# Sending one 2 MB zero fill as 17 narrow transfers and a rest

## The chip, the cores and the metric

The kernel runs on one core of one Trainium2 chip. The metric is device time in microseconds (us). Ratios are the mean time of one kernel's runs over the mean of the other's runs of the same rounds, so they are not quite the ratios of the medians that are quoted; 95% intervals stand beside them.

## The reference, cut to what matters

The reference is one decode step of a small transformer layer (sliding-window attention over a cache, then a gated unit) with its gradients. Only the last 4096 of 32768 cache rows are read, so the gradients of both caches are zero in the first 28672 rows of each of 8 groups.

```python
k = jnp.repeat(k_cache[:, :, Sk - W:, :], rep, axis=1)     # W = 4096, Sk = 32768
v = jnp.repeat(v_cache[:, :, Sk - W:, :], rep, axis=1)
...
_out, _vjp = jax.vjp(_f, A_x, A_k_cache, A_v_cache, A_wq, A_wo, B_w_gate, B_w_up, B_w_down)
```

Writing those zeros is most of the traffic: 103 fills of 2 MB go through GpSimd's queue alone (216 MB), out of 334.76 MB in all.

## The kernel before

`zeros` is the first 8192 columns of a large on-chip array, of which only the first half stays zero throughout. A fill copies it to 2 MB of a gradient. Fills 0 to 41 read all of it. Fills 42 to 54 read the first half twice, because block 1's gate and up weights are loaded into the second half. The later fills wait for a memset that restores that half.

```python
HALF0, HALF1 = 42, 55
zeros = ar(0, ZW)                                  # ZW = 8192
wgu_off = [RB + 28 * KB, ZW // 2]                  # block 1's weights: second half of zeros
...
def send_fills(n0, n1, halves=False):
    for reg in fills[n0:n1]:
        if halves:
            ZQ.dma_start(out=reg.rearrange("p (k f) -> p k f", k=2), in_=zeros[:, 0:ZW // 2].unsqueeze(1).to_broadcast([128, 2, ZW // 2]))
        else:
            ZQ.dma_start(out=reg, in_=zeros)

send_fills(0, HALF0)
send_fills(HALF0, HALF1, True)
...                                                # attention: scores and moments of 8 groups
def load_block(n):                                 # gate: SyncE's queue, up: ScalarE's
    f0, nb, w, wgu, wd = block_views(n)
    for eng, i, wt in ((LD, 0, B_w_gate), (nc.scalar, 1, B_w_up)):
        eng.dma_start(out=wgu[:, 0:3, i, :], ...)
        eng.dma_start(out=wgu[0:DQ, 3, i, :], ...)
    LD.dma_start(out=wd, ...)

load_block(0)
load_block(1)
...
for n in range(len(BLOCKS)):                       # three blocks of the gated unit
    ...                                            # DVE's four reductions over wgu (line 428)
    if n + 2 < len(BLOCKS):
        load_block(n + 2)                          # block 2 takes block 0's place
    if n == 1:
        nc.vector.memset(ar(ZW // 2, ZW // 2), 0.0)
        send_fills(HALF1, len(fills))
```

The order of instructions on each engine is not the order of the text: a scheduler chooses it when the kernel is built. In the trace GpSimd's 103 transfers name eight semaphores in turn, and each from the ninth on is issued after the landing of the one eight places before it: the first landed at 17.57 us, and the ninth was issued at 17.86.

## Time and profile before

| | before |
|---|---|
| time, 2 runs | 798.55 and 799.08 us |
| span of the profiled run | 797.2 us |
| DMA engines' share (sum of the queues) | 99.6% |
| median time of a 16384 B packet | 611 ns |
| first and last of the 16 engines to finish | 785.9 and 795.6 us |

The page and the views that matter are shown and read in the prediction. The last row comes from the packet records. They do not name the engine, but 28,930 of the 29,365 packets start 3 or 4 ns before another one ends, so they can be strung into sixteen chains, and a chain is taken for an engine here. Where two engines end a packet within a few ns the chains can swap. Ends, idle gaps and sums over all engines are safe; what one engine did over a long time is not.

### The profile page before, as it was taken

To read this page: it belongs to the slowest core of one execution; us is meant where nothing else is said; L and a number is where in the kernel's file an instruction comes from. 1 tells how busy PE (TensorE), PEld (TensorE's weight loads), DVE (VectorE), ACT (ScalarE), POOL (GpSimd) and SP (SyncE) were. 2 spreads that over 40 slices of the span, in tenths; PEclk is the share of its full clock that TensorE was granted. 3 is DMA by queue.
4 is the path that set the end of the run, shared out by engine and by line. 5 is a ranking of instruction groups with operands and counts; after the bars stand their busy time and mean duration, and the time that the engine had idled before them with its cause. 6 is when DMAs were issued, how large, how long until landed. Compare 5 with 4: busy or idle time off the path is not lost.

```text
span 797.2 us, 7318 instructions
## 1 busy us (share of the span) xinstructions
PE 478.9 (60%) x2926; PEld 222.6 (28%) x2926; DVE 437.1 (55%) x629; ACT 196.0 (25%) x309; POOL 61.8 (8%) x112
## 2 busy tenths in 40 slices
PE   0459999999999999251409478684450553722000
PEld 0334434344344333121208334331220211310000
DVE  2116584765846782263690679579653784964000
ACT  0142314134132201010102126353330442534000
POOL 4000000010101111100210001010000000000000
PEclk9989999999999999555558779766555556765555
DMA  9999999999999999999999999999999999999995
GB/s 349 431 430 430 428 431 430 430 428 430 430 423 427 427 419 413 423 421 424 432 428 423 424 431 431 428 425 427 424 424 422 424 424 424 423 427 418 433 434 247
DMA packets 29352, 334.76 MB, mean 420 GB/s; under 512 B 2819, under 2 KB 5894, under 8 KB 7814
## 3 DMA queue, kind: packets, MB, share of 16 engines
q0 software_dynamic: 16496, 216.01, 64.0%
q1 hardware_dynamic: 11382, 116.68, 34.8%
q10 hardware_dynamic: 1440, 1.61, 0.6%
q8 instruction: 23, 0.38, 0.2%
q14 instruction: 11, 0.09, 0.0%
HBM read 53.69 MB, written 280.59 MB: 419 GB/s over the span
## 4 chain that ended last, share of the span: by engine, by line
PE 37%; DMA 32%; DVE 16%; ACT 4%; issue 2%; another core or an unknown queue 0%; SPq 0%; DVEq 0%; ACTq 0%
DMA out_dram<-arena 19%; PE M_ps L317 12%; PE ok_ps L320 7%; PE rows_ps L256 6%; PE tr_ps L253 4%; DMA dh_bc<-in_grad_out_dram 4%; DMA arena<-in_A_k_cache_dram 4%; DMA arena<-in_B_w_down_dram 3%; ACT arena L270 2%; DVE arena L635 2%; DVE arena L459 2%; PE dqb_ps L502 2%; DMA arena<-in_B_w_gate_dram 2%; DVE arena L650 2%; PE d_ps L643 2%
## 5 line engine op out<-in xcount | busy, mean ns | idle before, releaser
L312 DVE TENSOR_TENSOR arena<-arena,p_f 128x2048 bf16<-128x2048 bf16 x64 | 145.4, 2286 | 61.6 <-PE M_ps L317 61.5
L317 PE MATMUL M_ps<-arena 128*128 128x512 bf16 x512 | 128.9, 380 | 0.2 <-ACT arena L323 0.2
L643 PE MATMUL d_ps<-arena,rT 32*128 32x512 bf16 x256 | 46.6, 529 | 111.0 <-DVE arena L651 63.9
L253 PE MATMUL tr_ps<-ident_bf,arena 128*128 128x128 bf16 x1024 | 92.5, 242 | 19.6 <-ACT arena L611 11.2
L256 PE MATMUL rows_ps<-arena,vpad 128*16 128x512 bf16 x256 | 90.6, 451 | 19.9 <-DVE arena L613 14.6
L133 POOL DMA_DIRECT2D out_dram<-arena x90 | 48.6, 542 | 538.5 <-DMA out_dram<-arena 491.3
L253 PEld LDWEIGHTS <-arena 128*128 128x128 bf16 x1024 | 69.0, 108 | 73.8 <-issue 64.4
L270 ACT COPY arena<-tr_ps 128x1024 bf16<-128x1024 bf16 x64 | 61.8, 1015 | 64.7 <-PE tr_ps L253 64.7
L647 ACT CAST arena<-d_ps 128x512 bf16<-128x512 f32 x64 | 37.7, 589 | 128.4 <-PE d_ps L643 128.3
L320 PE MATMUL ok_ps<-arena 128*16 128x512 bf16 x256 | 63.8, 381 | 0.9 <-DVE arena L297 0.9
L317 PEld LDWEIGHTS <-arena 128*128 128x128 bf16 x512 | 43.3, 99 | 59.0 <-issue 23.2
L611 ACT COPY arena<-tr_ps 128x1024 bf16<-128x1024 bf16 x32 | 32.6, 1019 | 94.6 <-PE tr_ps L253 36.4
L650 DVE CAST arena<-d_ps 128x512 bf16<-128x512 f32 x64 | 43.8, 684 | 16.9 <-PE d_ps L643 16.4
L651 DVE CAST arena<-d_ps 128x512 bf16<-128x512 f32 x64 | 43.5, 679 | 11.2 <-DMA out_dram<-arena 11.2
L643 PEld LDWEIGHTS <-rT 32*128 32x128 bf16 x256 | 11.2, 96 | 136.5 <-issue 90.0
L648 ACT CAST arena<-d_ps 128x512 bf16<-128x512 f32 x64 | 38.1, 595 | 11.9 <-DMA out_dram<-arena 11.9
L635 DVE TENSOR_TENSOR arena<-R_sb,tl_f 128x4096 bf16<-128x4096 bf16 x8 | 35.4, 4419 | 0.7 <-ACT R_sb L633 0.7
L256 PEld LDWEIGHTS <-vpad 128*16 128x16 bf16 x256 | 19.1, 92 | 58.4 <-issue 51.3
L320 PEld LDWEIGHTS <-arena 128*16 128x16 bf16 x256 | 19.1, 89 | 41.6 <-issue 20.5
L514 DVE CUSTOM_DVE_ANT_0 arena<-arena 128x4096 bf16<-128x4096 bf16 x3 | 13.1, 4423 | 23.9 <-ACT arena L507 23.9
L285 ACT ACTIVATE e_f<-cols_ps,nbias 128x32 f32<-128x32 f32 x16 | 4.5, 286 | 86.8 <-DVE nbias L281 86.8
L258 DVE COPY arena<-rows_ps 16x512 f32<-16x512 f32 x16 | 10.8, 676 | 26.6 <-PE rows_ps L256 26.6
(198 smaller groups left out, 387.9 us busy)
## 6 DMA issues: line engine op xcount, KB each, us to landing
out_dram<-arena POOLq DMA_DIRECT2D x103, 2048.0 KB, 51.7
out_dram<-arena SPq DMA_DIRECT2D x18, 2048.0 KB, 32.3
arena<-in_A_v_cache_dram SPq DMA_DIRECT2D x10, 2048.0 KB, 50.0
arena<-in_A_k_cache_dram SPq DMA_DIRECT2D x8, 2048.0 KB, 29.2
out_dram<-arena SPq DMA_DIRECT2D x4, 4096.0 KB, 43.8
arena<-in_A_wq_dram SPq DMA_DIRECT2D x2, 3072.0 KB, 20.6
arena<-in_A_wo_dram SPq DMA_DIRECT2D x2, 1792.0 KB, 14.5
out_dram<-arena SPq DMA_DIRECT2D x2, 1792.0 KB, 15.1
```

The source lines that it names most:

```text
L133: ZQ.dma_start(out=reg, in_=zeros)
L253: nc.tensor.transpose(tr_ps[:, dh, i, :], X_sb[:, 4 * q + i, dh * 128:(dh + 1) * 128], ident_bf[:])
L256: nc.tensor.matmul(rows_ps[:], lhsT=pad[:, dh, 16 * q:16 * q + 16], rhs=XT[:, dh].rearrange("p t k -> p (t k)"), start=(q == 0 and dh == 0 ...
L270: sT_ps = dots(kv_at(K_off[g]), KT_slot, vpad[g % 2], rows1, ps_c, "cols", lambda q, XT, ps: nc.scalar.copy(out=XT, in_=ps))
L312: nc.vector.tensor_tensor(out=pK, in0=K_sb[:, 4 * c:4 * c + 4, :].unsqueeze(2).to_broadcast([128, 4, 2, Dh]), in1=p_f[:, c::8, :].unsqueez ...
L317: nc.tensor.matmul(M_ps[:, vh, :], lhsT=V_sb[:, t, vh * 128:(vh + 1) * 128], rhs=pK[:, i, :, :].rearrange("p h d -> p (h d)"), start=(t == ...
L320: nc.tensor.matmul(ok_ps[:].rearrange("p k d -> p (k d)"), lhsT=ppad[g % 2][:, 8 * (t % 4) + t // 4, :], rhs=both(g, t), start=(g == 0 and ...
L635: nc.vector.tensor_tensor(out=RB_, in0=R_sb[:].unsqueeze(1).to_broadcast([128, 8, 512]), in1=tl_f[:].unsqueeze(2).to_broadcast([128, 8, 51 ...
L643: nc.tensor.matmul(d_ps[:, qi].rearrange("p w d -> p (w d)"), lhsT=rT[32 * q:32 * (q + 1), :], rhs=RB_[32 * q:32 * (q + 1), l, :], start=T ...
L648: nc.scalar.copy(out=stK[:, t:t + 2, :], in_=d_ps[:, :, 1, :])
L650: nc.vector.tensor_copy(out=stV[:, t:t + 2, :], in_=d_ps[:, :, 0, :])
L651: nc.vector.tensor_copy(out=stK[:, t:t + 2, :], in_=d_ps[:, :, 1, :])
```

## The change

The diff says what it does and not why. It sends fill 4 as seven transfers of 2 rows and ten of 3 rows, of 17 different lengths (1024 to 14848 B a row, 310,784 B in all), and the rest as 128 rows of 13956 B. A likely intent is to put the DMA engines out of step with one another.

```diff
-    send_fills(0, HALF0)
+    send_fills(0, 4)
+    flat = fills[4].rearrange("p f -> (p f)")
+    base = 0
+    for k, sizes in ((2, [512 * (17 + 2 * j) // 2 for j in range(7)]), (3, [512 * (1 + j) for j in range(5)]), (3, [256 * (11 + j) for j in range(5)])):
+        span = sum(sizes)
+        view = flat[base:base + k * span].rearrange("(k s) -> k s", k=k)
+        base += k * span
+        c0 = 0
+        for w in sizes:
+            ZQ.dma_start(out=view[:, c0:c0 + w], in_=zeros[0:k, 0:w])
+            c0 += w
+    rest = (128 * ZW - base) // 128
+    ZQ.dma_start(out=flat[base:].rearrange("(p f) -> p f", f=rest), in_=zeros[:, 0:rest])
+    send_fills(5, HALF0)
     send_fills(HALF0, HALF1, True)
```

## The prediction

> **What bounds the kernel now.** I read the page first: busy shares and the slices.
>
> ```profile
> PE 478.9 (60%) x2926; PEld 222.6 (28%) x2926; DVE 437.1 (55%) x629; ACT 196.0 (25%) x309; POOL 61.8 (8%) x112
> ...
> DMA  9999999999999999999999999999999999999995
> GB/s 349 431 430 430 428 431 430 430 428 430 430 423 427 427 419 413 423 421 424 432 428 423 424 431 431 428 425 427 424 424 422 424 424 424 423 427 418 433 434 247
> ```
>
> No compute engine passes 60%, but the DMA engines are full in every slice but the last. The queue table gives 64.0 + 34.8 + 0.6 + 0.2 = 99.6% of sixteen engines' span. In the packet records a packet of 16384 B takes 611 ns in the median, 26.8 GB/s per engine and 429 GB/s for sixteen. 334.76 MB at 429 GB/s is 780 us of the 797.2 us span, so at most 17 us can be won by any change that moves the same bytes. Where are they? Adding up each packet's time above the usual time for its size gives 9 us per engine, of which 1.9 us fall in the first 20 us. The rest is mostly start and end: all sixteen engines are busy until 785 us, then 14, 10 (at 788), 3 (at 790), 2 until 794, and the last stops at 795.6 us. Their mean end is near 789.3 us. That is an uneven finish of some 6 us.
>
> Second, GpSimd's queue and its waits.
>
> ```profile
> POOL out_dram L133 <- DMA out_dram<-arena: 491.3, 75, 9.6
> POOL out_dram L131 <- DMA out_dram<-arena: 76.4, 13, 9.3
> POOL out_dram L133 <- DVE arena L433: 35.6, 1, 35.6
> ```
>
> The built order says that each fill waits for the one eight places before it, so eight are under way: 16 MB of work that fills whatever the loads leave. The one other wait is for the memset of line 433, which makes the second half of the zero buffer again after block 1's gate and up weights have lain in it. Third, the timeline there:
>
> ```profile
> 341.62 0.67 POOL L131 DMA_DIRECT2D out_dram<-arena  x1 [5.33 <-DMA out_dram<-arena]
> 377.90 3.17 POOL L133 DMA_DIRECT2D out_dram<-arena  x6 [35.61 <-DVE arena L433]
> 381.69 0.53 POOL L133 DMA_DIRECT2D out_dram<-arena  x1 [0.63 <-DMA out_dram<-arena]
> 386.69 0.53 POOL L133 DMA_DIRECT2D out_dram<-arena  x1 [4.46 <-DMA out_dram<-arena]
> ```
>
> Nothing is issued from 341.62 to 377.90 us. Six then go at once, so only two old fills were left. In the packet records the old ones (packets of 8192 B) end at 380 us on the first engine and about 385 us on the last: the sixteen are 4.65 us apart there. **The reserve is 2.5 to 7 us**, and this is where the kernel is sensitive.
>
> [...] The trace has 1648 four-byte packets in GpSimd's queue, 103 x 16[...]. [...] from 354 to 362 us the three queues had 325, 326 and 325 packets, and since fills move 8192 B and weights 1280 B per packet, the weights get only about 28% of the engines' time.
>
> **The change, part by part.** Bytes stay the same. Added: 17 transfers, so 17 x 16 x 9 ns / 16 = 0.15 us of semaphore packets per engine, and 17 x about 0.54 us = 9 us on GpSimd, which is 8% busy. [...] As a direct effect: 0 +- 0.5 us.
>
> Two indirect effects are larger.
>
> *Part A, a thin fill queue near 40 to 49 us.* With eight under way, the first eight are now four fills and four small ones. Fill 3 landed at 42.06 us before. After it GpSimd still issues ten small or cut transfers, 10 x 0.54 = 5.4 us, before much data is queued, so the fills pause for about 9 us (data end 39 us, new data near 49 us). The loads have a backlog and take the whole rate. No time is lost there; the fills only fall behind by 9 x 0.215 = 2 MB. What it gives is this:
>
> ```profile
> PE tr_ps L253 <- DMA arena<-in_A_k_cache_dram: 8.2, 3, 3.7
> ```
>
> TensorE waited 3.66 us at 55.5 us for the second K load. That load would now land near 48.5 us, so I expect the wait gone. TensorE then has next to no wait until 308 us, so block 0 of the middle part should run about 3.6 to 4 us earlier.
>
> *Part B, the order of the weight loads.* The instruction order of the two builds differs in one place besides the fills. Before, SyncE and ScalarE issue block 1's gate and up loads ahead of block 2's. In the changed kernel block 2's come first, and they wait until DVE has finished block 0 (its four reductions of line 428).
>
> ```profile
> 309.95 0.38 SPq L356 DMA_DIRECT2D arena<-in_B_w_gate_dram  x1
> ...
> 344.60 0.33 SPq L358 DMA_DIRECT2D arena<-in_B_w_down_dram  x1
> 350.12 0.38 SPq L356 DMA_DIRECT2D arena<-in_B_w_gate_dram  x1
> 351.52 0.47 SPq L357 DMA_DIRECT2D arena<-in_B_w_gate_dram  x1
> ```
>
> 309.95 is block 1's gate load, 350.12 and 351.52 are block 2's. In the changed kernel block 1's load comes about 40 us later, behind block 2's. With part A block 0 ends near 347.5 us. Block 2's loads then start at about 346; data 3.4 us later (as 344.60 to 348.0 before), 12.5 us of packets (353.6 to 366.1 before): until 362. Block 1's are as many packets, 28 per engine and queue, of 1024 B: a round of three is 309 + 2 x 46 = 401 ns, so 11.2 us: until 373. Then, with durations from before: 32 matmuls of line 410, 3 us and more; copies, diagonals, broadcasts, 4.4 us; DVE's four reductions, 4.7 us; the memset, 1.8 us.
>
> ```profile
> 370.68 1.23 DVE L428 CUSTOM_DVE_ANT_0 arena<-arena 128x1024 bf16<-128x1024 bf16 x1 [0.37 <-issue]
> ...
> 375.84 1.76 DVE L433 MEMSET arena<- 128x2048 uint32 x1 [0.41 <-DVE hh_f L414]
> ```
>
> That puts the memset's end at 388 to 389 us instead of 377.6. GpSimd issues at once, and first data follow about 2.5 us later (377.9 to about 380.4 before): 391 to 392 us. The work that is queued without these fills is the same bytes as before, so the engines run dry at the same time: 380 us the first, 385 us the last. No other load is waiting (the next, line 461, was issued at 413.86). **So the DMA engines stand idle**, the first for some 11 us, the last for 6 to 7 us. The page's full rows would show a hole here.
>
> What counts at the end is the slowest engine. It loses 6 to 7 us, and the hole brings all engines level, which removes about 4.65 us of spread built up until then. The mean engine needed 789.3 - 382 = 407 us from here, the slowest 410.6. After the hole: 391.5 + 411 = 802.5 instead of 795.6, about **+7 us**. The compute chain is late by some 11 us too, but that is hidden: the last stores were issued from 731.88 us, while the work already queued would keep the engines full until about 803 - 33 = 770 us (14 MB come last, 33 us).
>
> Sum: 0.15 + 0 + 7 = +7, so 798.8 + 7 = about 806 us; I take 805.5 for a possible small gain from level engines.
>
> **Rivals.** *(1) Nothing runs dry.* If block 1's loads land some 5 us earlier than I reckon, or the fills' reserve is longer, only the fast engines pause, which costs nothing: 797 to 800 us. For it: the reserve of the slow engine is 7 us, and my sum has several terms of 3 to 12 us. *(2) The skew helps.* The rows may be meant to bring engines out of step so that they collide less. For it: 9 us of packet time above normal, and a 6 us uneven finish. Against: long packets are at 611 ns in the median and 622 ns at the 90th percentile, and most of the excess sits in a few moments when many loads begin. I would give it 3 to 6 us, so 792 to 796 us without the hole. *(3) Narrow transfers all start on the same engines*[...]: two engines get 131 KB instead of 19 KB, 4 us more. Alone this could give 802 us; with the hole, which levels the engines later, nothing more. *(4) A longer hole*: if part A's 3.6 us do not arrive, the restart is at 395 us, so 809 to 810 us.
>
> **Range and chances.** The main path gives 803 to 808, rival 1 about 798, rival 4 about 810. For 8 in 10 I take 799 to 811 us. Two per cent is 16 us: faster means under 782.8 us, which the 780 us of bytes plus start and landing all but rules out (1%). Slower means over 814.8 us and needs a hole of 16 us on the slowest engine (4%). Within 2%: 95%.
>
> **What the changed profile would show.** Right: GpSimd's issues of small rows at about 42 to 47 us; no 3.66 us wait of TensorE for K near 55 us; block 1's gate load issued near 348 us after block 2's; GpSimd's wait for line 433 longer, ending near 388 us; a DMA slice between 378 and 398 us below 90% and clearly below 424 GB/s; thereafter the same rates and a last slice like that of before. Wrong: a DMA row full throughout with the time at 798 us (rival 1), or fewer slow packets and a shorter uneven finish (rival 2), or the restart before 385 us.

The sum came to 0.15 + 0 + 7 = about +7 us, taken as 805.5 us. The second, 0 +- 0.5 us: how narrow rows are shared out among the engines was shown by no trace of the kernel before, so this term stands as my estimate alone. The 0.15 us rests on that kernel's trace: each fill has 16 four-byte packets of 9 ns (1648 for 103), and the semaphores that the fills name got as many updates (208 for 13 fills on seven of the eight, 192 for 12 on the last). The round of three packets in part B rests on the counts 325, 326 and 325 that are given there.

## The result, and the profile after

The changed kernel took 804.66 and 804.74 us, median 804.70, against 798.82: ratio 1.0073 (1.0049 to 1.0098). The changed kernel's line numbers are 13 higher than those of the kernel before. All outputs are right.

First the two DMA rows of the page of the changed kernel (forty slices of 20 us):

```profile
DMA  9999999999999999999799999999999999999997
GB/s 352 428 427 431 429 430 430 429 429 421 428 424 418 430 420 405 428 420 418 294 426 394 430 430 429 429 427 425 423 424 425 423 424 426 426 423 416 434 430 322
```

There is one hole, in the slice from 381 to 401 us: 294 GB/s, where the kernel before has 432. Slice 22 (421 to 442 us) is also low, at 394.

GpSimd's waits (for what, total us, times, longest):

```profile
POOL out_dram L133 <- DVE arena L446: 45.6, 1, 45.6
POOL out_dram L144 <- DMA out_dram<-arena: 38.4, 13, 8.4
```

The wait for the memset (line 446 here) grew from 35.6 to 45.6 us. The timeline of GpSimd (start, duration, what, idle before):

```profile
41.12 0.50 POOL L144 DMA_DIRECT2D out_dram<-arena  x1 [6.63 <-DMA out_dram<-arena]
42.34 0.51 POOL L144 DMA_DIRECT2D out_dram<-arena  x1 [0.72 <-DMA out_dram<-arena]
...
48.29 0.50 POOL L144 DMA_DIRECT2D out_dram<-arena  x1 [1.20 <-DMA out_dram<-arena]
50.01 0.50 POOL L144 DMA_DIRECT2D out_dram<-arena  x1 [1.22 <-DMA out_dram<-arena]
...
55.09 0.56 POOL L147 DMA_DIRECT2D out_dram<-arena  x1 [0.84 <-DMA out_dram<-arena]
```

and later:

```profile
342.18 0.67 POOL L131 DMA_DIRECT2D out_dram<-arena  x1 [4.32 <-DMA out_dram<-arena]
388.46 4.21 POOL L133 DMA_DIRECT2D out_dram<-arena  x8 [45.62 <-DVE arena L446]
395.89 0.53 POOL L133 DMA_DIRECT2D out_dram<-arena  x1 [3.21 <-DMA out_dram<-arena]
```

The small transfers go out every 1.1 to 1.7 us, so the wide rest of fill 4 is held back until 55 us, and the next full fill until 56.03. At 388.46 all eight places are free: the queue was empty. Why so late, SyncE's issues show:

```profile
347.48 0.38 SPq L369 DMA_DIRECT2D arena<-in_B_w_gate_dram  x1
348.88 0.52 SPq L370 DMA_DIRECT2D arena<-in_B_w_gate_dram  x1
349.70 1.24 SPq L369 DMA_DIRECT2D arena<-in_B_w_gate_dram  x1
351.14 1.32 SPq L370 DMA_DIRECT2D arena<-in_B_w_gate_dram  x1
```

The first two are block 2's, the last two block 1's, which was issued at 309.95 before. TensorE waits for them, by its list of waits in the stretch from 320 to 390 us, and the memset follows on DVE's timeline:

```profile
PE gu_ps L423 <- DMA arena<-in_B_w_gate_dram: 31.6, 2, 30.5
```

```profile
386.40 1.76 DVE L446 MEMSET arena<- 128x2048 uint32 x1 [0.41 <-DVE gu_f L424]
```

The memset ends at 388.16 us, against 377.60 before. Last, the stretches around it, first of the kernel before and then of the changed one; the last two columns are the DMA engines' share and GB/s. A packet counts whole in the stretch in which it starts, so a short stretch can show a share above 1.00 and a rate above that of whole slices:

```profile
380.00:385.00 5.00, 2.65 (x19) 2.06 (x19) 3.39 (x10) 1.77 (x3) 1.60 (x4) 0.50 1.02 436
385.00:390.00 5.00, 0.69 (x2) 0.10 (x1) 3.65 (x6) 0.76 (x2) 0.53 (x1) 0.50 1.02 438
```

```profile
380.00:385.00 5.00, 4.55 (x44) 3.33 (x43) 3.75 (x7) 0.65 (x2) 0.00 (x0) 0.50 0.59 247
385.00:390.00 5.00, 0.40 (x2) 0.16 (x3) 4.58 (x12) 0.00 (x0) 1.54 (x3) 0.50 0.22 93
390.00:395.00 5.00, 4.19 (x25) 2.44 (x23) 4.14 (x10) 1.77 (x3) 2.67 (x6) 0.50 1.01 393
```

In the packet records the engines run dry between 380.3 and 387.8 us and all start again at 389.6. They are idle 1.8 to 9.5 us each, 6.05 us in the mean. The last engine ends at 801.3 us instead of 795.6, the mean engine at 798.2 instead of 789.2. The sum for the mean engine closes: of these 9.0 us, 6.05 are the idle time, 2.7 are packets that took longer than the median for their size (11.45 us per engine over the run instead of 8.78; called excess below), and 0.3 are 500 added four-byte packets of 9 ns (2148 in GpSimd's queue instead of 1648).

### The profile page after: what moved, and what is told of

Same layout as the page of the kernel before. It is cut to its first block, busy times and chain, and to the rows that moved or that the text cites. A ratio compares the mean times of both kernels' runs of the same rounds, so it can differ in the third digit from the quotient of the medians.

```text
span 802.9 us, 7331 instructions
## 1 busy us (share of the span) xinstructions
PE 478.8 (60%) x2926; PEld 221.5 (28%) x2926; DVE 437.3 (54%) x629; ACT 195.8 (24%) x309; POOL 69.9 (9%) x129
## 5 line engine op out<-in xcount | busy, mean ns | idle before, releaser
L266 PE MATMUL tr_ps<-ident_bf,arena 128*128 128x128 bf16 x1024 | 90.8, 239 | 14.8 <-ACT arena L624 9.7
L423 PE MATMUL gu_ps<-X_b,arena 128*128 128x1 bf16 x112 | 9.7, 186 | 32.7 <-DMA arena<-in_B_w_gate_dram 31.6
```

Source lines behind the costliest of these rows:

```text
L266: nc.tensor.transpose(tr_ps[:, dh, i, :], X_sb[:, 4 * q + i, dh * 128:(dh + 1) * 128], ident_bf[:])
```

## The experiments

The theory: the time is lost in the hole, and the hole comes from the new order of the weight loads, which the rows only brought about through the scheduler. The rival: the rows themselves cost it. Both can be tested because the order can be pinned with ordering edges (no wait is removed). The order differs by more than the weight loads: some instructions of TensorE, DVE and ScalarE around the three blocks moved too, and the edges switch all of that together. The first four kernels ran on one chip in the same rounds as nine runs of the kernel before (median 798.94 us, 798.7 to 799.35), the next three, on that chip 15 minutes later, are compared with nine runs of the same median, eight of them the same executions as for the first four.

### e1: the rows, with the old order

```diff
+    def behind(dma, key):            # ordering edge only
+        if key in issued:
+            tc.add_manual_dep(dma.ins, issued[key].name, DependencyInfo(NoSync, DATA), ...)
     def load_block(n):               # block 2's loads go behind block 1's on each queue,
...                                   # and ScalarE's copies of block 0 behind block 1's up load
```

The resulting order on TensorE, DVE, ScalarE and SyncE is, instruction for instruction, that of the kernel before.

> The changed kernel with its 17 small rows, but with the instruction order of the kernel before on TensorE, DVE, ScalarE and SyncE (block 1's weight loads before block 2's, forced by ordering edges). Theory (the loss is the hole in the DMA row that the new order of the weight loads makes): no hole, DMA row full, the memset's end near 374 us, 798 to 800 us, ratio to before 0.999 to 1.002. Rival (the rows themselves cost it, by skew between the engines, by the pause of the fills or by 0.15 us and more of small packets): 803 to 805 us, ratio 1.005 to 1.008.

Measured: median 800.86 us (799.8 to 802.76, 5 runs), ratio 1.0027 (1.0015 to 1.0040). The memset ended at 374.39 us, and the stretches show no hole:

```profile
380.00:385.00 5.00, 1.78 (x10) 0.76 (x7) 2.52 (x4) 1.51 (x4) 0.53 (x1) 0.50 1.05 446
385.00:390.00 5.00, 0.51 (x2) 0.50 (x2) 4.37 (x8) 0.00 (x0) 0.53 (x1) 0.50 0.98 421
```

So most of the loss goes with the order. Some 1.9 us stay, a little more than I had allowed.

### e2: plain fills, with the new order

```diff
-    load_block(0)
-    load_block(1)
+    load_gu(0); load_down(0); load_down(1)
...
-                load_block(n + 2)
+                load_down(2); load_gu(2); load_gu(1)      # pinned by ordering edges
```

On the four engines this is, instruction for instruction, the order of the changed kernel.

> The kernel before with plain fills, but with the changed kernel's instruction order on TensorE, DVE, ScalarE and SyncE (block 2's weight loads before block 1's). Theory: a hole as in the changed kernel, and longer, since block 0 does not come 4 us earlier: memset's end near 392 us instead of 388, restart near 393.5, mean idle of an engine near 10 us instead of 6; 807 to 810 us, ratio 1.010 to 1.014. Rival (the rows themselves): 798 to 800 us, ratio 1.000.

Measured: median 807.31 us (806.93 to 807.54, 4 runs), ratio 1.0105 (1.0091 to 1.0119). The memset ended at 391.00 us, and fills came again at 392.4:

```profile
380.00:385.00 5.00, 3.83 (x22) 1.56 (x23) 2.77 (x8) 1.29 (x4) 0.00 (x0) 0.50 0.47 195
385.00:390.00 5.00, 2.38 (x28) 2.11 (x28) 4.59 (x10) 0.00 (x0) 0.00 (x0) 0.50 0.01 5
390.00:395.00 5.00, 2.02 (x5) 0.46 (x5) 4.90 (x16) 0.51 (x1) 3.70 (x8) 0.50 0.52 210
```

The mean idle time of an engine was 9.93 us, and the sum closes again: the mean engine ended 11.7 us later than before, 9.93 of idle time and 1.8 of excess. The order alone, without a single small row, makes the kernel slower than the change does. The two by two, in medians:

| | old order | new order |
|---|---|---|
| plain fills | 798.94 | 807.31 (e2) |
| small rows | 800.86 (e1), 800.43 (e7) | 804.70 (the change) |

Beside the new order the rows save 2.6 us, since their pause lets block 0 come earlier and the memset end 2.8 us sooner. (The cell of the change was measured beside other runs of the kernel before, at 798.82 us.)

### e3: the changed kernel with a longer reserve

```diff
-HALF0, HALF1 = 42, 55
+HALF0, HALF1 = 42, 58
```

> The changed kernel, order untouched, but 16 instead of 13 fills read only the first half of the zero buffer, so three more of them need not wait for the memset. Theory (an empty fill queue for some 6 us): those three fill it with about 15 us of work; DMA row full near 385 us; 798 to 800 us, ratio to before 1.000, though the weight loads come as late as in the changed kernel and the compute chain stays some 10 us late. Rival (late weights cost through the compute chain, or the rows cost by themselves): 803 to 805 us.

Measured: median 801.66 us (799.7 to 803.03, 5 runs), ratio 1.0034 (1.0021 to 1.0048). Block 1's weights come as late as in the changed kernel (TensorE waited 31.1 us for them at longest, the memset ended at 387.67), yet there is no hole:

```profile
380.00:385.00 5.00, 4.06 (x42) 3.19 (x41) 4.24 (x7) 0.65 (x2) 0.00 (x0) 0.50 1.00 421
385.00:390.00 5.00, 0.89 (x3) 0.34 (x4) 4.55 (x13) 0.00 (x0) 2.03 (x4) 0.50 1.01 424
```

So the loss comes from the empty queue; the late weights cost nothing through the compute chain that could be seen in runs 3 us apart. The time is above the 800 us that I gave and near that of e1, which also has the rows and no hole.

### e4: the control for e3

The same edit on the kernel before; no other instruction moves.

> Control: the kernel before with 16 instead of 13 such fills; no other instruction moves. Theory: it had no hole, so nothing is gained: 798 to 799.5 us, ratio 0.999 to 1.001. Rival (fast engines already ran dry there unseen, and that costs): 795 to 797 us.

Measured: median 799.62 us (798.85 to 800.43, 5 runs), ratio 1.0009 (0.9996 to 1.0021). There was nothing to gain, as expected; the median is 0.1 us above the range that I gave.

### e5, e6, e7: what the rows cost by themselves

All three have the old order. e5 sends the same bytes as transfers of 16 rows, which I took to give every engine the same share; that was not shown. e6 makes all narrow rows equally long, e7 is e1 again.

```diff
-    for k, sizes in ((2, [512 * (17 + 2 * j) // 2 for j in range(7)]), (3, ...), (3, ...)):
+    for k, sizes in ((16, [572] * 15 + [566] * 2),):                    # e5
+    for k, sizes in ((2, [3520] * 7), (3, [3520] * 10)):                # e6
```

> As the first experiment (small rows, old instruction order), but each of the 17 small transfers has 16 rows of 1144 or 1132 B[...]; the same 310,784 B. It keeps the thin fill queue and the earlier block 0[...]. If the uneven shares cause the 1.7 to 2 us that the first experiment was above the kernel before: 798.5 to 799.3 us, ratio 0.999 to 1.001, and engines ending as in the kernel before (last near 795.6 us). If the pause of the fills and what it moves causes it: 800 to 802 us, ratio 1.002 to 1.004.

> As the first experiment, but the 44 narrow rows are all 7040 B long, still on two or three engines each. If seventeen different lengths matter in themselves (phase between engines): different from the first experiment by over 1 us. If not: the same as the first experiment, 800 to 802 us, ratio 1.002 to 1.004. If the narrow transfers ran on the same engines each time[...], two engines would get 17 rows, 4.5 us of work, and the ends of the engines would differ by some 4 us more than in the kernel before.

> The first experiment again, beside the two others on one chip, since its runs ranged over 3 us: 800 to 802 us, ratio 1.002 to 1.004. Only if it differs from the two beside it by more than their ranges is there an effect of the lengths or shares.

Measured: e5 799.40 us (799.02 to 799.96, 5 runs), ratio 1.0006 (0.9993 to 1.0020); e6 799.71 us (798.78 to 801.78, 6 runs), ratio 1.0016 (1.0003 to 1.0029); e7 800.43 us (799.75 to 800.90, 4 runs), ratio 1.0018 (1.0005 to 1.0032). With 16 rows to a transfer (e5) no cost can be told from zero. Narrow rows cost about 0.2%. Whether their lengths differ makes no difference outside the scatter. e5 was 0.1 us above its first case, and e6 0.3 us below its range. The intervals of e5 and the others overlap, so the times alone do not show that the uneven shares are the cause.

e6 showed more in its packet records. All narrow rows there have one size, and their starts (ns from the span's start) fall into three series with steps of 1.48 and now and then 0.88 us: 39771, 41255, 42738, 43621 and so on, 17 rows; 41068, 42551, 43433 and so on, 17 rows; and from 48132 another ten, one for each 3-row transfer. These are as many as the transfers have first, second and third rows (17, 17 and 10), so I read them as row 0, row 1 and row 2 of every transfer, each always on the same engine. The changed kernel's own records agree for its seven 2-row transfers, each of another length: strung into chains, the seven first rows lie on one chain (from 39.525, 41.070, 42.652 us and so on) and the seven second rows on another (from 40.782, 42.326, 43.308 us and so on). By this reading the narrow transfers do not take turns, and in the changed kernel two engines carry 131,072 B of narrow rows and a third 48,640 B. The mean is 19,424 B, so the two would be (131,072 - 19,424) / 26.8 GB/s = 4.2 us behind, an estimate. The ends agree: in e1, e6 and e7 four engines end late (795.1 to 797.7 us; in e3 three, 795.7 to 797.4), where the kernel before has two (794.1 and 795.6) and e5 two (796.2 and 796.4). My expectation for e6 looked only at the difference between first and last end, 9.6 us against 9.7 before, which would have hidden this: the two loaded engines seem to have come level with two that were late anyway. A rival stays beside the uneven shares: in e1, e5, e6 and e7 the mean engine also ends 1.6 to 2.0 us later than before, much of it excess (see "What stays open" below), in e5 with a last end only 0.8 us later.

### e8 and e9: can narrow transfers relieve the late engines?

If row n went to engine n, which the records do not show, a fill on few engines could even out the end. e8 sends most of fill 4 as nine transfers of 14 full rows, e9 as eleven of seven.

```diff
+    for n in range(9):                                       # e9: 11 times, 7 rows
+        ZQ.dma_start(out=flat[base:base + 14 * ZW].rearrange("(k s) -> k s", k=14), in_=zeros[0:14, :])
+        base += 14 * ZW
```

> Old instruction order. In the packet records of the experiments so far the narrow rows do not move on round the engines: of the 17 equal rows two engines carried 17 each and a third 10, at a steady spacing[...]. This run sends most of the fifth fill as nine transfers of 14 rows of 16384 B: if row n goes to engine n, engines 0 to 13 carry 0.7 us more than with a plain fill and engines 14 and 15 carry 9 x 16384 B less of it, 4.9 us. If the two engines that end last in the kernel before (794.1 and 795.6 us, the rest by 791.1) are these two, the last end falls to about 791.5 and the time to 795 us, ratio 0.995. If only one or none of them is: 799 to 800.5 us, ratio 1.000 to 1.002. If narrow transfers did take turns on the engines: no change, ratio 1.000.

> Old instruction order. The fifth fill as eleven transfers of seven rows of 16384 B and a rest on all engines. If row n goes to engine n, engines 0 to 6 carry 3.8 us more than with a plain fill and engines 7 to 15 carry 2.9 us less. If both late engines of the kernel before are among 7 to 15: last end 792.5 to 793.5, 796 us, ratio 0.996 to 0.997. If one of them is among 0 to 6: last end near 799.5, 803 us, ratio 1.005. If narrow transfers took turns: 11 x 7 rows spread to within one row, no change, ratio 1.000.

Measured, with nine runs of the kernel before at a median of 798.88 us: e8 808.16 us (807.5 to 810.47, 4 runs), ratio 1.0121 (1.0108 to 1.0135); e9 812.83 us (809.4 to 813.5, 5 runs), ratio 1.0177 (1.0163 to 1.0190). Both attempts failed, and worse than any of my cases. In e9 nine engines end by 794.5 us and seven between 797.2 and 806.1, which agrees with seven rows on seven fixed engines; no engine of the nine is very late, so the late ones of the kernel before seem to be among the seven. Something else went wrong too. This is the row of the page of e8:

```profile
GB/s 352 427 312 412 430 430 429 431 428 428 430 423 427 426 420 410 424 420 410 419 428 411 425 429 432 426 423 427 424 424 425 422 424 427 424 424 418 431 436 247
```

In the third slice, where the narrow rows go, the rate is 312 GB/s, against 427 and 412 beside it, and packets take longer than usual. These are packets of GpSimd's queue alone: from 50 to 55 us its packets of 16384 B take 1382 ns in the median in e8 and 1378 in e9, and the loads' beside them 611. The longest rows of the changed kernel, 14848 B and two to a transfer, took 554 ns each. From 20 to 400 us the excess sums to 9.3 us per engine in e8 and 6.4 in e9, against 2.6 in the kernel before. The memset came late as well (383.7 and 383.5 us), so some engines ran dry, 1.4 and 2.9 us in the mean. Why GpSimd's packets took longer was not tested. So these two do not settle how much of their loss is the uneven share. No version beat the kernel before.

## Why the prediction was right or wrong

**What bounds the kernel, and the reserve: right.** e2 and e3 show from both sides that the time is lost where the fill queue runs empty, and no cost of the late compute chain shows beside it. One reading was off: in the packet records of the kernel before, the last engine ends its old fills at 385.9 us and not at 385, so the reserve was 2.5 to 8 us. The last stores were issued from 742.66 us instead of 731.88, and no slice between the hole and the end of the kernel shows idle engines.

**Part A: right in what it did, its pause was mis-sized.** TensorE's second wait for K went, and the last group's result came at 304.17 us instead of 308.20, 4.0 us earlier (predicted 3.6 to 4). But I paced the small transfers by GpSimd's issue time, 0.54 us each, and so put the rest's issue at 47.5 us. They went out every 1.1 to 1.7 us, and the rest at 55.09. No wide fill packet started between 39.2 and 59.0 us, so the pause was 20 us and not 9. Each transfer was issued after the landing of the one eight before it, and in the chains the packets of GpSimd's queue and of the loads' take turns (from 40 to 55 us only 8 of 830 neighbouring pairs are of one queue). So a row waits for load packets: from the first row at 39.525 us to the next on its chain at 41.070 there are, from start to start, the row (0.325 us) and two load packets (0.607 us each) with a four-byte packet between them (0.006). The spacing of 1.48 us in e6 is likewise one row (0.267 us) and two load packets (0.608 us each), and that of 0.88 fits one. The small transfers landed about 10 us after issue. It cost next to nothing, as the loads used the rate (424 to 426 GB/s from 40 to 60 us, 431 before).

**Part B: right, but its sum is wrong as written.** The memset's end was predicted at 388 to 389 us and came at 388.16. The terms listed give only 387: weights until 373, then 3 + 4.4 + 4.7 + 1.8 = 13.9 us. The weights' last packets ended at 374.3, and from there to the memset's end it took 13.9 us. So the steps were right, and it was luck that a margin which no term accounts for matched weights 1.3 us later than predicted. The orders of the two builds also differ in more than the one place that the prediction names, as said above. First data were predicted 2.5 us after the issue, so at 391 to 392, and came 1.1 us after it, at 389.6. The 2.5 us I had read off the kernel before was the time until the first engine had finished its old fills, not a latency.

**The hole and its effect on the slowest engine: the sum right, two terms off.** I had 11 us on the first engine and 6 to 7 on the last; measured were 9.5 and 1.8. The restart was 2 us earlier than predicted, and the last engine ran dry at 387.8 instead of 385 us (385.9 in the kernel before). From the restart to the end the slowest engine needed 411.7 us (predicted 411), so the end was 389.6 + 411.7 = 801.3 us instead of 802.5. That it lost 5.7 us though idle for only 1.8 is explained by the rest of the step: the hole made all engines start level, so the end is set by the restart and not by the engine that ran dry last.

**"A possible small gain from level engines": half right.** The uneven finish did shrink: the last end lies 3.1 us after the mean, against 6.4. But packets took longer after the hole. Between 380 and 400 us the excess was 0.62 us per engine instead of 0.02, and in the 20 us from the issue of the next large load (the query weights, at 413.86 us before and 423.34 after) 1.27 instead of 0.49. e2, which has a hole and no rows, shows 0.54 and 1.18; e1 and e3, which have rows and no hole, 0.05 and 0.64 to 0.73. So it goes with the hole. That level engines get in each other's way would explain it but is not shown: e9, where only some engines ran dry, has 1.13 at that load.

**The direct effect of the rows, "0 +- 0.5 us": wrong.** The packet records fit what rival 3 described: three series of 17, 17 and 10 rows in e6, and in the changed kernel the seven 2-row transfers on the same two chains, hence an estimated 131 KB on two engines. That rival's size for the rows alone, 802 us, compares with 800.86 and 800.43 in e1 and e7, and its claim that the hole would then level it agrees with the total. That 131 KB on an engine is what makes e1 and e7 slower stays argued, from the late ends above.

**Rivals.** Rival 1 (nothing runs dry) falls with the stretches. Rival 2 (out of step means fewer collisions) falls for this change: from 20 to 400 us the excess was 3.6 us per engine with the rows and no hole (e1), against 2.6 in the kernel before. Rival 4 (without part A, 809 to 810 us) describes e2, where it was 807.31.

What stays open: why e1, e5, e6 and e7 all have 1 to 1.3 us more excess per engine between 20 and 400 us than the kernel before (single profiles; e4, without rows, also has 0.8 more), e5 without any clear loss of time; how the 0.2% of the narrow rows divides between this and the uneven shares; and which engines are the late ones.

## What to carry to other kernels

When every slice of the DMA row is full, look for the place where a queue is refilled under a condition, and work out how many microseconds of work it then still holds: here that reserve (2.5 to 8 us in the kernel before, whose wait was 35.6 us) said how late the condition could come. Compare the built order of instructions on every engine before blaming or praising an edit, since a scheduler may answer an edit in one queue with a new order in another; pinning the order by edges separates the two. Look in the packet records for where transfers of few rows go: here 44 equal rows (e6) came in three series of 17, 17 and 10, and four engines ended late (795.1 to 797.7 us in e1, e6 and e7) where the kernel before has two. That the one causes the other stays argued.
